# GpSimd's opening work in written order, and each q tile's scaling tied behind a spread, in a fused attention and expert kernel

## The chip, the cores and the metric

The kernel runs on one core of a Trainium2 chip. The metric is device microseconds of one execution: 626.1 us as the median of three runs (622.59, 626.1 and 626.88). The engines are called as the profile calls them: PE (TensorE), DVE (VectorE), ACT (ScalarE), POOL (GpSimd), and SP, whose queue issues most of the transfers.

## The reference

Three layers follow each other. Attention works on batch 2, 8 heads, 768 positions, head size 64, with a distance bias, a local window of 96 and 8 global keys:

```python
scores = scale * np.matmul(q, k.transpose(0, 1, 3, 2))
keep = is_global | is_local
scores = np.where(keep, scores + bias[None], -1000000000.0)
a = np.exp(scores - np.max(scores, axis=-1, keepdims=True))
a = a / (np.sum(a, axis=-1, keepdims=True) + 1e-09)
attn = np.matmul(a, v)                        # 1536 tokens x 512
h = x @ w_in                                  # 512 x 2048
x2 = (h * np.tanh(softplus(h))) @ w_out
...                                           # argmax routing over 8 experts
out[mask] = gate_w[mask, None] * (np.maximum(xe @ w1[e], 0.0) @ w2[e])
```

## The kernel before

**Tiles.** The 1536 tokens are 12 tiles of 128 (`t`), six per batch. Attention of a tile takes two steps (`s = 2t` and `2t + 1`), one for each four heads. The dense layer works on blocks of two tiles and pairs of weight columns; it is interleaved with attention from step 5 on, goes on alone until about 395 us, and the experts follow.

**One attention step.** `a_S` multiplies scaled q by k on PE (tile `sp`). `a_max` on DVE adds the distance bias `ndist` and finds the row maximum, `a_exp` on ACT takes the exponential and sums the rows into `su`, `a_T` transposes on PE (`pt`), `a_Tev` copies to SBUF on ACT (`PT`), and `a_V` multiplies by v on PE (`av`). After the second step of a tile, `a_recip` inverts the row sums on DVE (L315, L316) and POOL *spreads* them over 64 columns per head into the tile `rs` (L318). `a_R` transposes `rs` on PE (`rb`, L324), ACT copies it back (L325), and `a_x` multiplies `av` by it on DVE (L385), rounds it to `xh` on ACT (L386) and writes the rest `xl` on DVE (L387). There is one `rs` buffer: the spread of a tile can be written only when L387 of the tile before has read it.

**Scaling of q.** `prep_qk(t)` multiplies a q tile in place by a power of two per head (L261), which `a_S` of that tile needs. Tile 0 is done on DVE, tiles 1 to 11 on POOL. q is loaded for tile 0, tile 1, and from then on for two tiles at a time (tile name `qr`). In the program's text `prep_qk(t)` stands one step ahead of its `a_S`. For the first tile of each batch it also copies the global keys inside `kT` (L258, L259).

**Bias.** `ndist` is built on DVE (`bias_part`) in two pieces and completed by four copies on POOL (`bias_copies`, L98 to L101). The first two copies need the first piece, L100 and L101 the second.

**What sets the order.** A tile framework records the instructions and orders each engine's queue by a scheduler, from priorities and an estimate of readiness; each engine then runs its queue strictly in that order and waits on semaphores. A block under `tc.manual_schedule()` keeps the order of the text for the engines it covers; the opening (steps 0 to 4, with some repeated `warm` matmuls between, L839) is such a block. As built, POOL's work was not kept in that order: the scheduler had hoisted the scalings as early as their data could be ready. SP issues loads in its own order; many wait for a free slot of the six `st` buffers that q tiles and raw weights (`wst`) share, and a slot comes free when DVE has converted its weights (L165, L167, L169, into `cv`, then ACT's L203 and DVE's L205 into `wpair`).

Of the kernel before, what the change touches and what calls it, by code (L numbers as in the profile page):

```python
# [13 lines left out]
ALU = mybir.AluOpType  # L14
# [4 lines left out]
B, H, S, D = 2, 8, 768, 64  # L19
# [6 lines left out]
NL, NG = 96, 8  # L26
NPRE = NL + NG
WN = NPRE + 128
# [13 lines left out]
def moe_kernel(ctx, tc, q, k, v, n_global, n_local, w_in, w_out, w_gate, w1, w2, out, dbg=None):  # L42
    nc = tc.nc
# [45 lines left out]
    def bias_iota(nd, ci):  # L89
        ri = nd.bitcast(I32)  # L90
        nc.gpsimd.iota(ci, pattern=[[1, NG]], base=0, channel_multiplier=0)
        for c0, n, base_ in ((2 * WN, NG, 0), (2 * WN + NG, 128, 0), (0, NL, NL)):
            nc.gpsimd.iota(ri[:, c0:c0 + n], pattern=[[-1, n]], base=base_, channel_multiplier=1)
        nc.gpsimd.iota(ri[:, NL:NPRE], pattern=[[0, NG]], base=1 << 20, channel_multiplier=0)

    def bias_copies(nd):
        diag = nd[:, 2 * WN + NG:WC]
        nc.gpsimd.tensor_copy(nd[:, WN + NL:WN + NL + 128], diag)  # L98
        nc.gpsimd.tensor_copy(nd[:, NPRE:WN], diag)
        nc.gpsimd.tensor_copy(nd[:, WN:WN + NL], nd[:, 0:NL])  # L100
        nc.gpsimd.tensor_copy(nd[:, WN + NL + 128:2 * WN], nd[:, NL:NPRE])  # L101

    def bias_part(nd, gk, tmp, c0, w, gc):
        ri = nd.bitcast(I32)
# [23 lines left out]
    qsc = const.tile([128, 4], F32, name="qsc")  # L128
    cqs = const.tile([128, 1], F32, name="cqs")

    def build_scales():
        for p_ in range(4):
            nc.vector.memset(qsc[0:64, p_:p_ + 1], 2.0 ** (2 * p_ - 2))
            nc.vector.memset(qsc[64:128, p_:p_ + 1], 2.0 ** (2 * p_ - 1))
        nc.vector.memset(cqs, 2.0 ** -42)
# [79 lines left out]
    qkt = {}  # L215
# [7 lines left out]
    def load_qk(t, n=2):  # L223
        b, i = divmod(t, TPB)
        c0 = NG + (i // 2) * KB + (i % 2) * 128
        w = n * 128
        nc.sync.dma_start(kT[:, :, c0:c0 + w], k_t[:, :, t * 128:t * 128 + w])
        qr = stp.tile([128, 4, w], F32, tag="st", name="qr")
        nc.sync.dma_start(qr, q_t[:, :, t * 128:t * 128 + w])
        for j in range(n):  # L230
            qkt[t + j] = qr[:, :, j * 128:(j + 1) * 128]
# [21 lines left out]
    def prep_qk(t):  # L253
        i = t % TPB
        if i == 0:
            for j in range(1, 4):
                g0 = j * KB
                nc.gpsimd.tensor_copy(kT[:, :, g0:g0 + NG], kT[:, :, NG:2 * NG])  # L258
            nc.gpsimd.tensor_copy(kT[:, :, 0:NG], kT[:, :, NG:2 * NG])  # L259
        eng = nc.vector if t == 0 else nc.gpsimd  # L260
        eng.tensor_tensor(out=qkt[t], in0=qkt[t], in1=qsc.unsqueeze(2).to_broadcast([128, 4, 128]), op=ALU.mult)  # L261

    def geom(t):
        i = t % TPB
# [12 lines left out]
    rbs = {}  # L277
# [28 lines left out]
    def a_exp(s, q_):  # L306
        t, pr = divmod(s, 2)
        w = geom(t)[1]
        h = 4 * pr + q_
        nc.scalar.activation(out=Ps[s][:, q_, 0:w], in_=Ps[s][:, q_, 0:w], func=AF.Exp,  # L310
                             bias=mxs[s][:, q_:q_ + 1], scale=-1.0, accum_out=rcs[t][:, h:h + 1])

    def a_recip(t):
        su = rcs.pop(t)
        nc.vector.tensor_scalar_add(su, su, 1e-9)  # L315
        nc.vector.reciprocal(su, su)  # L316
        rbs[t] = at.tile([128, 4, 128], F32, tag="rs", name="rs", bufs=1)
        nc.gpsimd.tensor_copy(rbs[t].rearrange("p a (b c) -> p (a b) c", c=64),  # L318
                              su.unsqueeze(2).to_broadcast([128, H, 64]))

    def a_R(t):
        rb = ps.tile([128, 4, 128], F32, tag="b", name="rb")
# [492 lines left out]
    def next_raw():  # L815
        if nraw[0] < 32:
            load_raw(*chunks[nraw[0]])
            nraw[0] += 1
# [9 lines left out]
                    pass  # L828

    NS = 5  # L830
    with tc.manual_schedule(), tc.tile_pool(name="tmp0", bufs=1, side="right") as tmp0:
        build_scales()
        load_qk(0, 1)
        make_identity(nc, ident)
        warm = ps.tile([128, 512], F32, tag="b", name="warm")

        def fill(n_):
            for _ in range(n_):
                nc.tensor.matmul(warm[:, 0:128], lhsT=ident, rhs=ident, start=True, stop=True)  # L839

        fill(NWARM)
        ci = tmp0.tile([128, NG], I32, name="ci")
        bias_iota(ndist, ci)
        load_v(0)
        load_qk(1, 1)
        next_raw()
        load_v(1)
        load_qk(2)
        next_raw()
        next_raw()  # L850
        nl = make_int(nl_raw, "nl")
        ng = make_int(ng_raw, "ng")
        cf = tmp0.tile([128, NG], F32, name="cf")
        nc.vector.tensor_copy(cf, ci)
        gk = tmp0.tile([128, NG], F32, name="gk")
        nc.vector.tensor_scalar(out=gk, in0=cf, scalar1=ng, scalar2=None, op0=ALU.is_lt)
        for _ in bias_part(ndist, gk, tmp0, 2 * WN, NG + 128, 0):
            pass
        prep_qk(0)
        b1 = bias_part(ndist, gk, tmp0, 0, NPRE, NL)  # L860
        a_S(0)
        prep_qk(1)
        for q_ in range(4):
            a_max(0, q_)
        a_S(1)
        for s in range(NS):
            for q_ in range(2):
                a_exp(s, q_)
            if s:
                fill(4)  # L870
                a_T(s - 1, 0)
                a_T(s - 1, 1)
            if s and s + 1 < NS:
                a_S(s + 1)
            if s == 2:
                prep_qk(2)
            if s == 0:
                for _ in range(6):
                    next(b1, None)
            if s == 4:  # L880
                a_x(0)
            if s + 1 < NS:
                a_max(s + 1, 0)
                a_max(s + 1, 1)
            if s:
                a_Tev(s - 1, 0)
                a_Tev(s - 1, 1)
            if s in (2, 3):
                next_conv(1)
            for q_ in range(2, 4):  # L890
                a_exp(s, q_)
            if s + 1 < NS:
                a_max(s + 1, 2)
                a_max(s + 1, 3)
            if s == 0:
                for _ in range(6):
                    next(b1, None)
                bias_copies(ndist)
            if s in (1, 3):
                a_recip(s // 2)  # L900
            if s:
                fill(3)
                a_V(s - 1)
            if s in (2, 4):
                a_R(s // 2 - 1)
            if s in (2, 3):
                next_conv(2)
            if s in (1, 2):
                next_raw()
                next_conv(0)  # L910
            if s == 2:
                load_v(2)
            if s == 4:
                load_v(3)
        a_x(1)
        make_fast()
        build_consts(tmp0)
# [117 lines left out]
    for u in range(u0, NU + 2):  # L1035
        pl, bl, jl = units[u - 2]
        rt = bl - 1 if pl == 2 and bl > 0 else None
        if u < NU:
            p, b, j = units[u]
# [140 lines left out]
    with tc.If(slow > 0):  # L1180
        dense = nc.values_load(flag[0:1, 1:2], min_val=0, max_val=1)
        with tc.If(dense > 0):
            xd = dr.tile([NT, DM], F32, name="xd")
            sld = dr.tile([1, H], F32, name="sld")
            with tc.tile_pool(name="fa", bufs=1) as fa, tc.tile_pool(name="fap", bufs=1, space=PSUM) as fap:
# [13 lines left out]
                for b in range(B):  # L1199
                    with tc.For_i(0, H, 1) as hi_:  # L1200
# [10 lines left out]
                        for i in range(TPB):  # L1211
# [27 lines left out]
                            su = fa.tile([128, 1], F32, name="fsu")  # L1239
# [152 lines left out]
```

## Time and profile before

| | us |
|---|---|
| median of three runs | 626.1 |
| lowest and highest run | 622.59, 626.88 |
| the profiled execution | 625.67 |
| its span, first to last instruction | 623.9 |
| PE busy | 588.4 (94%) |
| DVE busy | 477.1 (76%) |
| ACT busy | 379.9 (61%) |
| POOL busy | 93.5 (15%) |

Busy times are of one profiled execution. In the 40 slices of the page, PE is at 9 tenths or more nearly everywhere from about 90 us on; the slices below that lie in the opening and where the experts begin. The mean clock granted to TensorE was 0.982 of full speed. A busy PE is not a PE at its peak: the record of a matmul also lasts longer when the granted clock is lower.

### The profile page before, as it was taken

What the parts mean: (1) busy time and instruction counts of PE and PEld (TensorE: products, weight loads), DVE (VectorE), ACT (ScalarE), POOL (GpSimd) and SP (SyncE); (2) the same over time, 40 slices, a digit from 0 to 9 for tenths busy, and PEclk for the clock granted to TensorE, in tenths of its full rate; (3) what the DMA queues carried; (4) which work ended last, traced back from release to release, by engine and by line L of the source; (5) the groups of instructions that cost most, each with busy time, mean ns of one, the idle gap of its engine ahead of it and who ended that gap; (6) DMA issues with size and microseconds to landing.
All of it is one profiled execution on the core that took longest, in us unless ns stands there. A gap on an engine that the chain in (4) does not pass through costs nothing.

```text
span 623.9 us, 12022 instructions
## 1 busy us (share of the span) xinstructions
PE 588.4 (94%) x4326; PEld 524.8 (84%) x4326; DVE 477.1 (76%) x1143; ACT 379.9 (61%) x882; POOL 93.5 (15%) x167
## 2 busy tenths in 40 slices
PE   7988799999999999999999999998999999999991
PEld 6766677777788999998989889788999999999990
DVE  5888899995579999877767677755985777988741
ACT  3659688977767666555555555555664566777630
POOL 2232120000100100000201111121310212221111
PEclk9979899999999999999999999999999999999996
DMA  7865656579959565441322210277667376568000
GB/s 216 296 187 185 200 187 231 207 246 285 271 192 319 177 217 188 136 136 35 103 92 78 86 52 34 98 251 270 209 222 256 107 270 229 174 241 301 28 17 20
DMA packets 54903, 109.93 MB, mean 176 GB/s; under 512 B 5707, under 2 KB 12875, under 8 KB 54834
## 3 DMA queue, kind: packets, MB, share of 16 engines
q1 hardware_dynamic: 49138, 90.18, 43.6%
q0 software_dynamic: 5696, 18.89, 9.1%
q8 instruction: 36, 0.59, 0.4%
q14 instruction: 33, 0.27, 0.1%
HBM read 84.64 MB, written 25.10 MB: 176 GB/s over the span
## 4 chain that ended last, share of the span: by engine, by line
PE 71%; DVE 9%; DMA 6%; ACT 6%; issue 4%; POOL 2%; SPq 0%; DVEq 0%; POOLq 0%; ACTq 0%
PE hp L418 22%; PE acc L437 18%; PE bhp L701 4%; PE bacc L701 4%; DMA bst<-in_moe_w_dram 3%; PE av L372 3%; PE bhp L702 2%; PE bacc L702 2%; DVE bw L155 2%; DMA xg<-x,dsi 1%; PE bhp L704 1%; PE bacc L704 1%; PE bacc L706 1%; PE bhp L706 1%; PE bacc L705 1%
## 5 line engine op out<-in xcount | busy, mean ns | idle before, releaser
L418 PE MATMUL hp<-xh,wpair 128*128 128x256 f32 x768 | 153.1, 289 | 3.3 <-ACT xh L386 3.3
L418 PEld LDWEIGHTS hp<-xh,wpair 128*128 128x128 f32 x768 | 123.4, 191 | 10.4 <-ACT xh L386 4.9
L437 PE MATMUL acc<-wpair,gh 128*128 128x512 f32 x384 | 123.1, 398 | 1.4 <-ACT gh L474 1.4
L418 PE MATMUL hp<-xl,wpair 128*128 128x256 f32 x384 | 111.9, 291 | 0.5 <-DVE xl L387 0.3
L437 PEld LDWEIGHTS acc<-wpair,gh 128*128 128x128 f32 x384 | 68.7, 188 | 16.5 <-issue 3.1
L155 DVE TENSOR_TENSOR bw<-bst,bw 128x512 fp32r<-128x512 f32 x112 | 72.9, 685 | 11.6 <-ACT bw L154 10.9
L445 ACT ACTIVATE e<-hp 128x512 f32<-128x512 f32 x48 | 28.7, 599 | 83.7 <-PE hp L418 83.6
L154 ACT CAST bw<-bst 128x512 fp32r<-128x512 f32 x112 | 64.3, 620 | 21.9 <-PE bhp L705 9.6
L437 PE MATMUL acc<-wpair,gl 128*128 128x512 f32 x192 | 76.9, 401 | 0.0
L418 PEld LDWEIGHTS hp<-xl,wpair 128*128 128x128 f32 x384 | 73.2, 191 | 3.2 <-DVE xl L387 1.4
L701 PE MATMUL bhp<-xc,bw 128*128 128x352 f32 (+4 forms) x192 | 59.4, 364 | 0.6 <-DVE t L736 0.5
L701 PE MATMUL bacc<-hc,bw 128*128 128x352 f32 (+4 forms) x192 | 59.3, 364 | 0.1
L310 ACT ACTIVATE P<-P,mx 128x232 f32<-128x232 f32 (+1 forms) x96 | 45.0, 470 | 18.0 <-DVE mx L299 18.0
L702 PE MATMUL bhp<-xc,bw 128*128 128x176 f32 (+4 forms) x192 | 48.4, 252 | 0.0
L702 PE MATMUL bacc<-hc,bw 128*128 128x176 f32 (+4 forms) x192 | 48.4, 252 | 0.0
L455 DVE SCALAR_TENSOR_TENSOR n<-n,r 128x512 f32<-128x512 f32 x48 | 33.6, 700 | 15.2 <-ACT r L453 15.1
L477 DVE SCALAR_TENSOR_TENSOR gl<-n,gh 128x512 fp32r<-128x512 f32 x48 | 33.6, 701 | 12.2 <-ACT gh L474 11.0
L437 PEld LDWEIGHTS acc<-wpair,gl 128*128 128x128 f32 x192 | 36.1, 188 | 7.3 <-DVE gl L477 0.2
L701 PEld LDWEIGHTS bhp<-xc,bw 128*128 128x128 f32 x192 | 36.1, 188 | 1.7 <-DVE t L736 0.7
L701 PEld LDWEIGHTS bacc<-hc,bw 128*128 128x128 f32 x192 | 36.1, 188 | 1.0 <-DVE hc L744 0.3
L702 PEld LDWEIGHTS bacc<-hc,bw 128*128 128x128 f32 x192 | 36.7, 191 | 0.0
L702 PEld LDWEIGHTS bhp<-xc,bw 128*128 128x128 f32 x192 | 36.7, 191 | 0.0
(190 smaller groups left out, 1252.0 us busy)
## 6 DMA issues: line engine op xcount, KB each, us to landing
bst<-in_moe_w_dram SPq DMA_DIRECT2D x56, 512.0 KB
wst<-in_moe_w_in_dram SPq DMA_DIRECT2D x16, 512.0 KB
wst<-in_moe_w_out_dram SPq DMA_DIRECT2D x16, 512.0 KB
xl<-xs POOLq DMA_DIRECT2D x12, 512.0 KB, 4.0
xh<-xs POOLq DMA_DIRECT2D x12, 512.0 KB, 4.7
xpl<-xps SPq DMA_DIRECT2D x24, 256.0 KB
xg<-z SPq DMA_DIRECT2D x24, 224.9 KB
w0f<-in_moe_w_dram SPq DMA_DIRECT2D x8, 512.0 KB
```

Source lines behind the costliest of these rows:

```text
L154: nc.scalar.copy(hi, src)
L155: nc.vector.tensor_sub(lo, src, hi.bitcast(F32))
L310: nc.scalar.activation(out=Ps[s][:, q_, 0:w], in_=Ps[s][:, q_, 0:w], func=AF.Exp, bias=mxs[s][:, q_:q_ + 1], scale=-1.0, accum_out=rcs[t][ ...
L372: nc.tensor.matmul(av[64 * j:64 * j + 64, 2 * pr + i, :], lhsT=lh, rhs=rh, start=(c == 0), stop=(c == 1))
L418: yield lambda f=f, kk=kk, wi=wi, xx=xx, cs=cs: nc.tensor.matmul(hp[:, f, :], lhsT=w[:, wi, kk, cs], rhs=xx[:, kk, :], start=(kk == 0 and ...
L437: yield lambda f=f, o=o, cs=cs, gi=gi, wi=wi, first=first, last=last: nc.tensor.matmul(accs[b][o], lhsT=gi[:, cs], rhs=w[:, wi, f, :], sta ...
L445: nc.scalar.activation(out=e, in_=hp, func=AF.Exp, scale=-1.0)
L455: nc.vector.scalar_tensor_tensor(out=n, in0=n, scalar=0.25, in1=r, op0=ALU.add, op1=ALU.mult)
L477: nc.vector.scalar_tensor_tensor(out=gl, in0=n, scalar=-(2.0 ** -80), in1=gh.bitcast(F32), op0=ALU.mult, op1=ALU.subtract)
L701: nc.tensor.matmul(o[:, 0:2 * cap], lhsT=wh, rhs=xc, start=first, stop=False)
L702: nc.tensor.matmul(o[:, 0:cap], lhsT=wl, rhs=xh, start=False, stop=last)
L704: nc.tensor.matmul(o[:, 0:cap], lhsT=wh, rhs=xh, start=first, stop=False)
```

## The change

Two things. The opening's `manual_schedule` now names PE, ACT, DVE and Pool, so POOL's instructions of the opening stand in the order of the text. And each scaling of a q tile from tile 3 on is traced in `tc.issue_after(...)`, which puts it on POOL's queue behind the instruction that `gorder` holds: the latest spread traced so far (`gorder` is first set to the last bias copy). No instruction is added or removed on any engine. PE, DVE and ACT have the same instructions in the same order. On SP one small load moves: `wg` (128x4x8 floats, 16 KB) now stands ahead of the k load of tiles 4 and 5 and no longer behind the first two stores to `xs`.

```diff
+    gorder = [None]
+
     def bias_copies(nd):
...
-        nc.gpsimd.tensor_copy(nd[:, WN + NL + 128:2 * WN], nd[:, NL:NPRE])
+        gorder[0] = nc.gpsimd.tensor_copy(nd[:, WN + NL + 128:2 * WN], nd[:, NL:NPRE]).ins
...
         eng = nc.vector if t == 0 else nc.gpsimd
-        eng.tensor_tensor(out=qkt[t], in0=qkt[t], in1=qsc.unsqueeze(2).to_broadcast([128, 4, 128]), op=ALU.mult)
+        with tc.issue_after(gorder[0]) if t > 2 else nullcontext():
+            eng.tensor_tensor(out=qkt[t], in0=qkt[t], in1=qsc.unsqueeze(2).to_broadcast([128, 4, 128]), op=ALU.mult)
...
-        nc.gpsimd.tensor_copy(rbs[t].rearrange("p a (b c) -> p (a b) c", c=64),
-                              su.unsqueeze(2).to_broadcast([128, H, 64]))
+        gorder[0] = nc.gpsimd.tensor_copy(rbs[t].rearrange("p a (b c) -> p (a b) c", c=64),
+                                          su.unsqueeze(2).to_broadcast([128, H, 64])).ins
...
-    with tc.manual_schedule(), tc.tile_pool(name="tmp0", bufs=1, side="right") as tmp0:
+    with tc.manual_schedule(engines={mybir.EngineType.PE, mybir.EngineType.Activation, mybir.EngineType.DVE, mybir.EngineType.Pool}), tc.tile_pool(name="tmp0", bufs=1, side="right") as tmp0:
```

The first place is POOL's queue in the opening, before the change. `qr_161` is the q load of tiles 2 and 3, `qr_568` that of tiles 4 and 5; `rs_286` and `rs_407` are the spreads of tiles 0 and 1.

```order
L98 COPY ndist_100<-ndist_100 128x128
L99 COPY ndist_100<-ndist_100 128x128
L261 TENSOR_TENSOR qr_161<-qr_161,qsc_95 128x4x128
L100 COPY ndist_100<-ndist_100 128x96
L101 COPY ndist_100<-ndist_100 128x8
L318 COPY rs_286<-su_212 128x512
L261 TENSOR_TENSOR qr_161<-qr_161,qsc_95 128x4x128
L261 TENSOR_TENSOR qr_568<-qr_568,qsc_95 128x4x128 x2
L318 COPY rs_407<-su_274 128x512
```

The same place now (line numbers are 2 or 3 higher in the changed file).

```order
L100 COPY ndist_100<-ndist_100 128x128
L101 COPY ndist_100<-ndist_100 128x128
L102 COPY ndist_100<-ndist_100 128x96
L103 COPY ndist_100<-ndist_100 128x8
L321 COPY rs_286<-su_212 128x512
L264 TENSOR_TENSOR qr_161<-qr_161,qsc_95 128x4x128
L321 COPY rs_407<-su_274 128x512
L140 MEMSET ones_89 128x128
L141 MEMSET tri_88 128x128
L264 TENSOR_TENSOR qr_161<-qr_161,qsc_95 128x4x128
```

The scaling of tile 2 moved from ahead of the last two bias copies to behind the spread of tile 0; the scalings of tiles 3, 4 and 5 no longer stand ahead of the spread of tile 1.

The second place is POOL's queue in the main loop, before the change: `qr_875` are tiles 6 and 7, `qr_1203` tiles 8 and 9, `qr_1520` tiles 10 and 11; the `rs` rows are the spreads of tiles 2 to 6.

```order
L318 COPY rs_589<-su_394 128x512
L258 COPY kT_104<-kT_104 128x4x8
L259 COPY kT_104<-kT_104 128x4x8
L261 TENSOR_TENSOR qr_875<-qr_875,qsc_95 128x4x128 x2
L318 COPY rs_742<-su_600 128x512
L258 COPY kT_104<-kT_104 128x4x8
L318 COPY rs_903<-su_753 128x512
L261 TENSOR_TENSOR qr_1203<-qr_1203,qsc_95 128x4x128 x2
L258 COPY kT_104<-kT_104 128x4x8
L261 TENSOR_TENSOR qr_1520<-qr_1520,qsc_95 128x4x128 x2
L318 COPY rs_1055<-su_914 128x512
L318 COPY rs_1224<-su_1066 128x512
```

The same place now.

```order
L321 COPY rs_589<-su_394 128x512
L264 TENSOR_TENSOR qr_568<-qr_568,qsc_95 128x4x128
L260 COPY kT_104<-kT_104 128x4x8
L261 COPY kT_104<-kT_104 128x4x8
L321 COPY rs_742<-su_600 128x512
L264 TENSOR_TENSOR qr_568<-qr_568,qsc_95 128x4x128
L260 COPY kT_104<-kT_104 128x4x8
L321 COPY rs_903<-su_753 128x512
L264 TENSOR_TENSOR qr_875<-qr_875,qsc_95 128x4x128
L260 COPY kT_104<-kT_104 128x4x8
L321 COPY rs_1055<-su_914 128x512
L264 TENSOR_TENSOR qr_875<-qr_875,qsc_95 128x4x128
```

The pairs of scalings came apart: one scaling stands behind each spread, that of tile t behind the spread of tile t - 2, and so on to tile 11 behind the spread of tile 9.

## Rows read from the trace of the kernel before

**Rows 1.** The page's first line.

```profile
span 623.9 us, 12022 instructions
```

**Rows 2.** Windows: length, then PE, PEld, DVE, ACT, POOL busy, clock, DMA share, GB/s.

```profile
15.00:20.00 5.00, 4.95 (x45) 3.69 (x43) 1.95 (x12) 1.78 (x8) 1.57 (x4) 1.00 1.05 374
20.00:25.00 5.00, 4.54 (x38) 3.17 (x40) 4.96 (x14) 2.96 (x10) 1.87 (x2) 1.00 0.55 168
...
30.00:35.00 5.00, 1.84 (x21) 1.17 (x20) 5.00 (x7) 2.54 (x7) 3.69 (x5) 0.99 0.42 152
35.00:40.00 5.00, 4.75 (x21) 3.67 (x21) 3.92 (x17) 3.29 (x9) 0.57 (x4) 0.50 0.81 256
...
110.00:120.00 10.00, 10.00 (x84) 7.89 (x82) 9.76 (x25) 8.59 (x24) 0.92 (x1) 1.00 0.38 127
...
200.00:300.00 100.00, 100.00 (x664) 90.70 (x664) 86.89 (x156) 58.76 (x101) 7.97 (x16) 1.00 0.45 147
```

**Rows 3.** The chain that ended last, in order of time: start, length, what.

```profile
32.53 1.48 POOL qr L261
...
57.82 1.03 POOL qr L261
```

**Rows 4.** Timeline of POOL: start, length, instruction, idle before and its releaser.

```profile
16.57 1.04 POOL L261 TENSOR_TENSOR qr<-qr,qsc 128x512 f32<-128x512 f32 x1 [5.15 <-DMA qr<-in_q_dram]
17.56 0.26 POOL L100 COPY ndist<-ndist 128x96 f32<-128x96 f32 x1
...
31.31 2.71 POOL L261 TENSOR_TENSOR qr<-qr,qsc 128x512 f32<-128x512 f32 x2 [9.44 <-DMA qr<-in_q_dram]
...
42.08 0.61 POOL L318 COPY rs<-su 128x512 f32<-128x512 f32 x1 [0.99 <-PE pt L337]
...
56.58 2.28 POOL L261 TENSOR_TENSOR qr<-qr,qsc 128x512 f32<-128x512 f32 x2 [6.06 <-DVE su L315]
...
82.23 2.49 POOL L261 TENSOR_TENSOR qr<-qr,qsc 128x512 f32<-128x512 f32 x2 [0.81 <-DMA qr<-in_q_dram]
...
99.88 0.87 POOL L318 COPY rs<-su 128x512 f32<-128x512 f32 x1 [10.93 <-DVE su L316]
```

**Rows 5.** Timeline of DVE.

```profile
13.58 0.27 DVE L119 TENSOR_TENSOR ndist<-loc,rel 128x104 f32<-128x104 f32 x1
...
17.98 0.40 DVE L299 CUSTOM_DVE_ANT_0 P<-sp,ndist 128x232 f32<-128x232 f32 x1 [4.14 <-POOL ndist L101]
...
30.99 0.69 DVE L387 TENSOR_TENSOR xl<-rs,xh 128x512 fp32r<-128x512 f32 x1
31.59 1.53 DVE L167 SCALAR_TENSOR_TENSOR cv<-wst,cv 128x512 int32<-128x512 int32 x1
...
45.65 0.43 DVE L447 TENSOR_SCALAR e<-e 128x512 f32<-128x512 f32 x1 [1.14 <-ACT e L445]
...
57.48 0.19 DVE L316 RECIPROCAL su<-su 128x8 f32<-128x8 f32 x1
...
61.70 0.40 DVE L299 CUSTOM_DVE_ANT_0 P<-sp,ndist 128x232 f32<-128x232 f32 x1 [1.15 <-PE sp L286]
```

**Rows 6.** One line's instructions in 0 to 60 us: minimum, median, maximum in ns.

```profile
L167 DVE SCALAR_TENSOR_TENSOR cv<-wst,cv x8: 677/737/1532, 20.0 to 49.7; 128x512 int32<-128x512 int32 x8
```

**Rows 7.** Timeline of PE.

```profile
31.33 1.36 PE L372 MATMUL av<-PT,vv 104*64 104x128 f32 x16 [0.98 <-ACT PT L350]
...
34.82 1.08 PE L324 MATMUL rb<-ident,rs 128*128 128x128 f32 x4 [2.13 <-POOL rs L318]
...
55.80 1.05 PE L286 MATMUL sp<-kT,qr 64*128 64x232 f32 x8
...
59.46 0.66 PE L324 MATMUL rb<-ident,rs 128*128 128x128 f32 x4 [1.60 <-POOL rs L318]
...
91.44 0.88 PE L372 MATMUL av<-PT,vv 128*64 128x128 f32 x12 [0.76 <-ACT PT L350]
...
113.76 1.05 PE L286 MATMUL sp<-kT,qr 64*128 64x232 f32 x8
```

## The prediction

> **What bounds the kernel now.** I read the windows first. From 110 us PE is busy in the whole of its time, and in 200 to 300 us it is busy 100.00 of 100 [rows 2]; whatever brings PE to that stretch earlier shortens the run by as much. In the opening it is different. In 30 to 35 us PE is busy 1.84 of 5, and in the next five its granted clock is 0.50, the lower of its two levels, 1.2 GHz [rows 2]. So the change has to be priced in the opening, from about 14 to 100 us.
>
> Next the chain of waits. It runs twice through POOL's scaling of q: at 32.53 us, and at 57.82 us [rows 3]. Both times the scaling stands ahead of a spread in POOL's queue, and PE waits for the spread: 2.13 us at 34.82 and 1.60 us at 59.46 [rows 7]. These scalings are of tiles 4 to 7, which nobody needs yet.
>
> Third, the timelines of POOL and DVE. At 16.57 POOL has waited 5.15 us for a q load; two small bias copies stand behind that, and DVE waits 4.14 us for them until 17.98 [rows 4, 5]. So three waits in the trace are of one kind: something short and urgent behind a scaling.
>
> The sum is made against the profiled execution, 625.67 us, of which the span is 623.9 [rows 1]; that run lies 0.4 us below the median of the three, 626.1.
>
> **The change part by part.** Nothing is added on an engine; eleven POOL scalings remain eleven.
>
> *Term A, the bias copies.* DVE has written the second bias piece at 13.58 + 0.27 = 13.85 us [rows 5]; the copies, which began at 17.56 [rows 4], can begin there, 3.7 us earlier. That is the upper end. But PE, with its warm matmuls in fixed order, is busy 4.95 of 5 and 4.54 of 5 in 15 to 25 us [rows 2]: it can gain only its idle time, 0.05 + 0.46 = 0.5 us. I take **0.5**, the PE end, because the next step of attention needs PE. What DVE gains beyond it is a head start for term B.
>
> *Term B, the spread of tile 1.* It follows the scalings of tiles 4 and 5, which take 31.31 to 34.02 [rows 4]. Now it only needs the buffer `rs`, free when DVE's L387 ends: 30.99 + 0.69 = 31.68 us [rows 5]. PE finishes `av` at 31.33 + 1.36 = 32.69 and waits until 34.82 [rows 7]; with the spread ready by then the whole **2.13** goes. That `av` had itself waited 0.98 us for ACT's copy of PT [rows 7], late because ACT had to wait for DVE before it; DVE's head start of term A should remove it too: **0.98** (ends 0 and 0.98).
>
> *Term C, the clock.* The clock fell right after these two waits of PE. In 35 to 40 us PE was busy 4.75 us at half speed [rows 2]; at full speed the same work takes 2.4, so up to 2.4 us come back, and nothing if DVE sets the pace. DVE is busy 3.92 of those 5 us [rows 2], and at 45.65 it waits 1.14 us for ACT, which had waited for the slow matmuls [rows 5]. I take **1.1**, what DVE itself waited.
>
> *Term D, the spread of tile 3.* The reciprocal is ready at 57.48 + 0.19 = 57.67 us [rows 5]; the spread had to let two scalings end at 56.58 + 2.28 = 58.86 [rows 4]. That is 1.2 us; PE's wait was 1.60, and DVE's for the scores behind it 1.15 at 61.70 [rows 5, 7]. I take **1.1** (ends 0 and 1.6).
>
> *Term E, what the scalings cost where they now stand.* While POOL scales, some DVE instructions take longer: L167 took 1.53 us beside the pair at 31.31, and 0.68 undisturbed [rows 5, 6]. One scaling therefore costs DVE between 0 and 0.85 us. Before, the pair of tiles 4 and 5 fell into PE's wait and cost nothing that counts. Now tiles 3, 4 and 5 follow spreads where DVE is nearly full: up to 2.6, of which DVE's remaining waits cover a part; I take **-1.0**. Tiles 6 to 11 fall later, tile 8 behind the spread at 99.88 [rows 4] and the last three beyond 110 us, where PE is full (10.00 of 10 busy, DVE 9.76 [rows 2]): I take 0 for these six, and keep -0.85 apiece for the lower end. In return the pair at 82.23, 2.49 us long [rows 4], no longer lies in front of DVE's work there; PE waited 0.76 us for ACT at 91.44, downstream of it [rows 4, 7]: **+0.76**.
>
> The SBUF page of the Trainium skill ("SBUF — State Buffer", section "Who interferes with whom") states that the port pair which DVE and GpSimd share is an exclusive lock: the second to issue is blocked for the whole first instruction if it has two SBUF inputs. This speaks against the change: by it every scaling behind a spread would cost DVE a whole scaling; the sum would lose what the third rival below works out. The 1.53 us agree with a lock in kind, but 0.85 is less than one scaling.
>
> *Terms of nothing.* The delayed scalings are hidden: tile 4 is scaled behind the spread at 42.08 + 0.61, so by about 43.8 with a 1.04 us scaling, and its scores start at 55.80; tile 8 behind the spread at 99.88 + 0.87, so by 101.8, scores at 113.76 [rows 4, 7]. Twelve microseconds of cover each; if it went, each late microsecond would be one of PE's. The `wg` load moves ahead of one k load on SP; that k is first read at 55.80 too, and `wg` not before routing. The key copies keep their places relative to the spreads, and other loads keep their order on SP.
>
> **Sum:** 0.5 + 2.13 + 0.98 + 1.1 + 1.1 - 1.0 + 0.76 = 5.6 us, so 625.67 - 5.6 = **620.1 us**.
>
> **The rivals.**
>
> *DVE is the real bound of the opening (chance 0.20).* For it: DVE is busy 5.00 of 5 in the very window where PE waits, 30 to 35 us [rows 2]. Against it: its instructions there are early work, stretched by the scalings. Then only DVE's own waits count: 1.08 in 35 to 40, 1.14 and 1.15 [rows 2, 5], together 3.4, less one more disturbed scaling than before, 0.85. Gain 2.5: 623.2 us.
>
> *PE is the bound throughout (0.15).* Then each cost of term E vanishes, C counts 2.4 and D 1.6: 0.5 + 2.13 + 0.98 + 2.4 + 1.6 + 0.76 = 8.4, so 617.3 us. For it: PE is full from 110 us on. Against it: ACT and DVE in between.
>
> *The scalings block DVE in full, and it comes out slower (0.06).* Nine scalings (tiles 3 to 11) then each hold up DVE by 1.04 us [rows 4], 9.4 in all, directly behind the reciprocal, where DVE has work. Of the old ones, four lay in DVE's dense part (tiles 8 to 11), at 0.85 each: 3.4 go. Net loss 6.0, against the 3.4 of DVE's own waits from the first rival: 2.6 slower, 628.3 us. It decides once DVE's delay per tile exceeds what DVE has to spare: 0.24 of 10 us in 110 to 120 [rows 2]. Against it: PE, not DVE, has the fuller record there. This is what the lock rule of the Trainium skill's SBUF page, named under term E, would make of the change.
>
> **How the numbers follow.** The forecast has 0.59, with 618 to 622.5 as its own range. A difference of 1% is 6.3 us, so the line against the median lies at 619.8 us, a hair from my sum; such a bound is about what a measurement of this kernel can tell from no change. Some 45% of the forecast's chance lies beyond it, 0.27, with the second rival's 0.15: faster 0.42. Same: the rest of the forecast, the first rival and most of the third, 0.55. Slower by over 1% would need the third rival at its worst: 0.03. The range reaches down to the edge of the second rival and up through the first: 617 to 625.
>
> **What would show it.** Right: `ndist` copies near 14 us and DVE's wait of 4.14 gone (A); the transposes of `rs` for tile 1 without a wait on POOL, before 32 us (B); clock 1.00 from 30 to 45 us (C); the next wait of PE on POOL at 59.46 gone (D). PE should reach its first dense matmul (L418) some 3.6 us earlier. What is late next: ACT's `xh`, which follows DVE's L385. Wrong: PE now waits as long for ACT or DVE in the same places; DVE's conversions last 1.5 us behind every spread; `a_S` waits on POOL; or the clock drops after another wait.

## The result and the profile after

The changed kernel takes 619.81 us (median of 17 runs, 616.71 to 624.35), the kernel before 625.2 us beside it (17 runs, 622.59 to 630.88). The ratio is 0.991, 95% interval 0.9888 to 0.9932: the 5.4 us are real, and a little less than the 1% that the prediction set as its line. The forecast was 620.1 us. Two slow runs of variants further down (711.92 us with only the engines named, at a mean clock of 0.75, and 629.04 us with tiles 3 to 5 tied) are in none of the medians and ratios.

The profiled execution of the changed kernel took 619.42 us. Its page and windows (length, busy us of PE, PEld, DVE, ACT and POOL, clock, DMA share, GB/s), to be laid beside [rows 1, 2]:

```profile
span 617.6 us, 12020 instructions
...
15.00:20.00 5.00, 5.00 (x47) 3.77 (x44) 4.55 (x16) 3.32 (x12) 2.07 (x2) 1.00 1.07 364
...
30.00:35.00 5.00, 2.23 (x21) 1.46 (x18) 3.05 (x9) 2.37 (x6) 3.70 (x7) 1.00 0.57 164
35.00:40.00 5.00, 5.00 (x48) 4.51 (x47) 4.97 (x22) 3.40 (x11) 1.86 (x3) 1.00 0.79 283
```

DVE works through 15 to 20 us, where it had waited; PE is full at full clock in 35 to 40 us, where it had run at 0.50. But in 30 to 35 us PE is still idle for more than half of the time. POOL's timeline tells why (start, length, instruction, idle before and its releaser):

```profile
13.97 0.27 POOL L102 COPY ndist<-ndist 128x96 f32<-128x96 f32 x1 [2.54 <-DVE ndist L121]
...
16.82 1.48 POOL L264 TENSOR_TENSOR qr<-qr,qsc 128x512 f32<-128x512 f32 x1
29.52 2.46 POOL L321 COPY rs<-su 128x512 f32<-128x512 f32 x1 [11.22 <-DVE xl L390]
...
32.23 1.04 POOL L264 TENSOR_TENSOR qr<-qr,qsc 128x512 f32<-128x512 f32 x1
...
38.33 0.62 POOL L321 COPY rs<-su 128x512 f32<-128x512 f32 x1 [0.88 <-DVE su L319]
38.90 1.48 POOL L264 TENSOR_TENSOR qr<-qr,qsc 128x512 f32<-128x512 f32 x1
...
53.62 0.61 POOL L321 COPY rs<-su 128x512 f32<-128x512 f32 x1 [6.33 <-DVE su L319]
```

The bias copies stand at 14 us and each spread goes ahead of its scaling (that at 16.82 is tile 2's, long done when the spread of tile 1 starts), against [rows 4]. The new thing is the third row: the spread of tile 1 starts as soon as its buffer is free, with nothing in front of it, and lasts 2.46 us; the spreads at 38.33 and 53.62 last 0.61. DVE's timeline of the same microseconds, and the rows that answer to [rows 5]:

```profile
14.40 0.40 DVE L302 CUSTOM_DVE_ANT_0 P<-sp,ndist 128x232 f32<-128x232 f32 x1 [0.57 <-ACT PT L353]
...
29.29 0.68 DVE L169 SCALAR_TENSOR_TENSOR cv<-wst,cv 128x512 int32<-128x512 int32 x1
29.89 0.41 DVE L167 TENSOR_SCALAR cv<-wst 128x512 int32<-128x512 int32 x1
30.23 0.68 DVE L171 SCALAR_TENSOR_TENSOR cv<-wst,cv 128x512 int32<-128x512 int32 x1
30.83 0.68 DVE L169 SCALAR_TENSOR_TENSOR cv<-wst,cv 128x512 int32<-128x512 int32 x1
33.40 0.69 DVE L388 TENSOR_TENSOR rs<-av,rs 128x512 f32<-128x512 f32 x1 [1.90 <-ACT rs L328]
...
39.40 1.52 DVE L207 TENSOR_TENSOR wpair<-cv,wpair 128x512 fp32r<-128x512 f32 x1
```

DVE runs four weight conversions back to back from 29.29 to 31.51 us, none of them stretched, and the spread ends 0.47 us after the last, at 31.98. PE's timeline shows who pays:

```profile
29.29 1.10 PE L375 MATMUL av<-PT,vv 104*64 104x128 f32 x16
...
32.03 0.66 PE L327 MATMUL rb<-ident,rs 128*128 128x128 f32 x4 [1.65 <-POOL rs L321]
...
34.80 0.38 PE L421 MATMUL hp<-xh,wpair 128*128 128x256 f32 x1 [1.12 <-ACT xh L389]
...
43.71 0.44 PE L375 MATMUL av<-PT,vv 104*64 104x128 f32 x4 [1.15 <-ACT PT L353]
...
54.29 0.66 PE L327 MATMUL rb<-ident,rs 128*128 128x128 f32 x4 [0.63 <-POOL rs L321]
...
60.05 0.58 PE L421 MATMUL hp<-xh,wpair 128*128 128x256 f32 x1 [2.53 <-ACT xh L389]
```

The wait of 2.13 us [rows 7] is still there with 1.65, and DVE waits 1.90 us behind it at 33.40. In the chain of waits of the changed kernel (start, length, what) the spread has taken the scaling's place of [rows 3]:

```profile
29.52 2.47 POOL rs L321
```

By how much PE is earlier than before, in the two profiled executions (one of each kernel, both with the granted clock at 1.00 in 10 to 12 us):

| PE starts | before | after | earlier |
|---|---|---|---|
| scores of step 2 | 12.75 | 12.83 | -0.08 |
| scores of step 4 | 24.77 | 23.78 | 0.99 |
| transposes of `rs`, tile 1 | 34.82 | 32.03 | 2.79 |
| first dense matmul | 38.01 | 34.80 | 3.21 |
| scores of step 8 | 55.80 | 51.59 | 4.21 |
| scores of step 9, second part | 61.01 | 55.84 | 5.17 |
| scores of step 10 | 72.18 | 68.25 | 3.93 |
| scores of step 13 | 93.59 | 87.65 | 5.94 |
| transposes of `rs`, tile 11 | 170.87 | 165.50 | 5.37 |
| wait for `gh` near the end of the dense layer | 405.14 | 399.76 | 5.38 |
| end of the span | 623.9 | 617.6 | 6.3 |

### The profile page after: what moved, and what is told of

Same layout as the page of the kernel before. It is cut to its first block, busy times and chain, and to the rows that moved or that the text cites. A ratio compares the mean times of both kernels' runs of the same rounds, so it can differ in the third digit from the quotient of the medians.

```text
span 617.6 us, 12020 instructions
## 1 busy us (share of the span) xinstructions
PE 585.2 (95%) x4326; PEld 523.5 (85%) x4326; DVE 474.7 (77%) x1143; ACT 379.8 (61%) x882; POOL 93.9 (15%) x167
## 4 chain that ended last, share of the span: by engine, by line
PE 76%; DVE 7%; ACT 6%; DMA 5%; issue 3%; POOL 1%; SPq 0%; DVEq 0%; POOLq 0%; ACTq 0%
PE hp L421 23%; PE acc L440 18%; PE bhp L704 5%; PE bacc L704 5%; PE av L375 3%; PE bhp L705 2%; PE bacc L705 2%; DMA bst<-in_moe_w_dram 2%; DMA xg<-z 2%; PE sp L289 2%; ACT P L313 2%; PE warm L842 1%; PE bhp L707 1%; PE bacc L707 1%; PE bacc L709 1%
```

## The experiments

In all of them the kernel before ran on the same chip beside the variant, which has 4 to 10 runs. Beside the ratio of times with its interval stand three numbers of one profiled execution each, which need not be near the median: how long after the start of DVE's `xl` of tile 0 (L387 before, L390 now), which frees `rs`, the transposes of tile 1 begin on PE; when PE's matmul that waits for `gh` starts; and how long the spread of tile 1 lasts.

| kernel | median us | ratio [95%] | `xl` to transposes | `gh` wait | spread of tile 1 |
|---|---|---|---|---|---|
| before | 625.2 | 1 | 3.83 | 405.14 | 0.80, behind a pair |
| changed | 619.81 | 0.9910 [0.9888, 0.9932] | 3.34 | 399.76 | 2.46 |
| changed, again | 619.74 | 0.9911 [0.9882, 0.9939] | 3.37 | 400.42 | 2.46 |
| only the engines named | 625.94 | 1.0015 [0.9994, 1.0037] | 5.34 | 407.19 | 0.61, behind a pair |
| tile 3 tied | 625.24 | 1.0012 [0.9987, 1.0038] | 5.33 | 405.21 | 0.61, behind a pair |
| tiles 4, 5 tied | 623.42 | 0.9984 [0.9959, 1.0010] | 1.81 | 402.44 | 0.91 |
| tiles 3 to 5 tied | 621.8 | 0.9947 [0.9917, 0.9977] | 3.34 | 399.07 | 2.46 |
| scaled twice | 622.12 | 0.9949 [0.9924, 0.9975] | 3.35 | 402.25 | 2.46 |
| spread 1 on ACT | 617.71 | 0.9889 [0.9856, 0.9923] | 2.26 | 398.26 | 0.61, on ACT |
| fewer warm | 615.93 | 0.9887 [0.9835, 0.9939] | 1.81 | 398.12 | 0.91 |
| fewer warm, again | 618.29 | 0.9894 [0.9862, 0.9926] | 3.36 | 398.38 | 2.45 |
| fewer warm, spread on ACT | 618.25 | 0.9891 [0.9844, 0.9937] | 2.28 | 396.15 | 0.61, on ACT |
| no warm | 618.04 | 0.9874 [0.9846, 0.9902] | 3.35 | 400.35 | 2.45 |
| warm in step 9 | 619.18 | 0.9912 [0.9883, 0.9940] | 3.35 | 400.44 | 2.46 |

The column of `xl` sorts them: 1.81 where the spread lasts 0.91, 2.26 to 2.28 where ACT does it, 3.34 to 3.37 where it lasts 2.45 or 2.46, 5.3 where a pair of scalings that DVE holds up stands ahead of it, and 3.83 in the profile of before, where the pair got in between DVE's conversions.

**Which half of the change acts.** The naming of the engines alone, with no scaling tied:

```diff
-        with tc.issue_after(gorder[0]) if t > 2 else nullcontext():
+        with nullcontext():
```

> The other half of the change alone: the opening's manual schedule names its four engines, and no scaling is tied. GpSimd's queue comes out as it was before; only the wg load moves on SP's queue. Theory (naming the engines does nothing on GpSimd and wg's load is hidden): 624 to 626, ratio 1.000 within its interval, DVE's wait of 4.14 us and PE's of 2.13 us stay. Rival (the early wg load disturbs the full transfers of 8 to 20 us): 0.3% or more slower, later landings of q and raw weights.

It did nothing (1.0015). POOL's order in this kernel is that of before, the scaling ahead of the bias copies and the pair ahead of the spread. Its timeline, then rows of DVE's and PE's:

```profile
16.44 1.04 POOL L264 TENSOR_TENSOR qr<-qr,qsc 128x512 f32<-128x512 f32 x1 [5.04 <-DMA qr<-in_q_dram]
17.42 0.26 POOL L102 COPY ndist<-ndist 128x96 f32<-128x96 f32 x1
...
32.55 3.03 POOL L264 TENSOR_TENSOR qr<-qr,qsc 128x512 f32<-128x512 f32 x2 [10.80 <-DVE cv L167]
35.52 0.61 POOL L321 COPY rs<-su 128x512 f32<-128x512 f32 x1
```

```profile
32.99 0.68 DVE L169 SCALAR_TENSOR_TENSOR cv<-wst,cv 128x512 int32<-128x512 int32 x1
38.01 0.69 DVE L388 TENSOR_TENSOR rs<-av,rs 128x512 f32<-128x512 f32 x1 [4.33 <-ACT rs L328]
```

```profile
36.19 1.11 PE L327 MATMUL rb<-ident,rs 128*128 128x128 f32 x4 [3.62 <-POOL rs L321]
```

DVE's wait at 18 us stays (4.04), as expected, but PE's is 3.62 where the profile of before has 2.13. Here the pair ends 1.91 us after the last of DVE's four conversions (35.58 against 33.67), none of which is stretched; in the profile of before the pair got in between and stretched one to 1.53 [rows 5]. One order of the queue thus met with either result.

So the effect needs the tying of the scalings. The other kernels keep the naming of the engines; the tie without the naming wasn't run.

**Term by term.** Only some tiles are tied; the three conditions, one for each kernel:

```diff
-        with tc.issue_after(gorder[0]) if t > 2 else nullcontext():
+        with tc.issue_after(gorder[0]) if t == 3 else nullcontext():
+        with tc.issue_after(gorder[0]) if t in (4, 5) else nullcontext():
+        with tc.issue_after(gorder[0]) if t in (3, 4, 5) else nullcontext():
```

> Only the scaling of tile 3 is tied behind a spread; it was the one that stood ahead of the last two bias copies. The scalings of tiles 4 and 5 stay ahead of the spread of tile 1. Theory (bias copies are worth little because PE is full there; the spreads carry the gain): DVE's wait of 4.14 us at 18 us goes, PE's fourth score block starts about 1.0 us earlier, PE's wait for the spread of tile 1 at 34.82 us stays or grows to 3 us, and the time is 624.5 to 625.5, under 0.2% from before. Rival (DVE's head start is the gain): 621 to 622.5, half of the change or more.

> Only the scalings of tiles 4 and 5 are tied behind spreads; tile 3 still stands ahead of the bias copies. Theory: PE's 2.13 us wait for the spread of tile 1 shrinks to about 1.5 (DVE now locks the spread out for a while), the clock stays at 1.00 from 35 to 42 us, and the time is 621.5 to 623.5: 2 to 3.5 us of the 5.6. Rival (bias copies carry it): 624 to 625.5.

> Tiles 3, 4 and 5 are tied, 6 to 11 stay hoisted in pairs. Theory (terms A to C alone, without the moved scalings of tiles 6 to 11): the opening up to 53 us is as in the changed kernel; PE's wait for the spread of tile 3 (1.60 us before) comes back, DVE instructions of 1.2 to 1.5 us return near 75 and 80 us; 621 to 622.5. Rival (the scalings behind spreads cost DVE time in 88 to 142 us): faster than the changed kernel, 618 to 619.5.

With tile 3 alone the bias copies come at 13.96 us, and nothing is gained (1.0012). The timelines of POOL, PE and DVE of that kernel:

```profile
30.12 4.49 POOL L264 TENSOR_TENSOR qr<-qr,qsc 128x512 f32<-128x512 f32 x2 [10.93 <-DVE cv L167]
34.56 0.61 POOL L321 COPY rs<-su 128x512 f32<-128x512 f32 x1
...
35.42 1.04 POOL L264 TENSOR_TENSOR qr<-qr,qsc 128x512 f32<-128x512 f32 x1
```

```profile
35.22 1.11 PE L327 MATMUL rb<-ident,rs 128*128 128x128 f32 x4 [3.63 <-POOL rs L321]
```

```profile
32.04 0.68 DVE L169 SCALAR_TENSOR_TENSOR cv<-wst,cv 128x512 int32<-128x512 int32 x1
37.04 0.69 DVE L388 TENSOR_TENSOR rs<-av,rs 128x512 f32<-128x512 f32 x1 [4.33 <-ACT rs L328]
```

DVE's wait at 18 us is gone. But it waits 4.33 us at 37 us, as it does with only the engines named, and there too the pair ends 1.9 us after DVE's last conversion (34.61 against 32.72): these waits aren't brought by the tie. Against that execution, whose opening is the nearest (granted clock 0.50 in 10 to 12 us, here 0.64), `xl` starts 0.96 us earlier (29.89 against 30.85) and the transposes 0.97; why this isn't in the time isn't shown. The expected 1.0 us at the fourth score block didn't come: the scores of step 4 start at 24.98, against 24.77 before and 24.91 with only the engines named. This kernel shows also that the scaling ahead of the bias copies is tile 3's: tying tile 3 moves it away (now 35.42).

Tiles 4 and 5 alone give nothing in the time that can be told from none (0.9984, interval to 1.0010), though here the 2.13 us of term B went in full. PE's timeline of that kernel:

```profile
31.30 1.37 PE L375 MATMUL av<-PT,vv 104*64 104x128 f32 x16 [0.98 <-ACT PT L353]
32.77 0.66 PE L327 MATMUL rb<-ident,rs 128*128 128x128 f32 x4
```

The spread starts at 31.80 and lasts 0.91, and the transposes wait for nobody; `av` waits its 0.98 us as before [rows 7], and DVE still waits 4.06 us at 18 us. Tiles 3 to 5 together give 0.9947, more than the two parts' 1.0012 and 0.9984. That suggests that the two waits stand one behind the other and that their removal pays together, but the excess over the two parts, 0.005, is hardly larger than the noise of the three ratios together, so it isn't shown. As expected, PE waits again for the spread of tile 3, which here stands behind a pair: 1.60 us at 55.18, against 0.63 in the changed kernel. Whether tiles 6 to 11 add the rest, up to 0.991, isn't settled: the intervals touch, and in the trace this kernel is at the `gh` wait 0.7 us ahead of the changed one and loses 3.2 us in the expert stage after it (end of span 620.1), where no scaling is. Its granted clock there was 0.57 in 404 to 408 and in 428 to 432 us, against 1.00 in both in the changed kernel.

**What a scaling costs where it now stands.** Each scaling from tile 3 on is followed by a second one, by ones, also on POOL:

```diff
+            if t > 2:
+                eng.tensor_tensor(out=qkt[t], in0=qkt[t], in1=qone.unsqueeze(2).to_broadcast([128, 4, 128]), op=ALU.mult)
```

> The changed kernel, with each scaling of tiles 3 to 11 followed by a second multiplication by 1.0 on GpSimd: nine more instructions of about 1.04 us, each right behind a scaling. Theory (outside tiles 3 to 5 PE covers the disturbance of DVE): 0 to 1.5 us slower than the changed kernel, 620 to 621.5. Rival (each blocks DVE in full and DVE sets the pace): 5 to 9 us slower, 625 to 629.

622.12 us, 2.3 us above the changed kernel for nine more scalings: 0.26 us apiece. The two intervals overlap (0.9924 to 0.9932), so the size is loose. The time lies between the two expectations. The scalings neither leave DVE alone nor hold it up each time: of the 128x512 instructions of DVE up to 180 us that are recorded one by one, 8 last more than 1.1 us in this kernel and 3 in the changed one (6 before).

**Whether the 2.46 us of the spread are DVE's doing.** The spread of tile 1 is done by ACT, ahead of the transposes; all other spreads stay on POOL. The scaling tied to it moves to the spread of tile 0 (20.69 us).

```diff
+        if t == 1:
+            late[0] = su
+            return
...
     def a_R(t):
+        if t == 1:
+            rbs[t] = at.tile([128, 4, 128], F32, tag="rs", name="rs", bufs=1)
+            nc.scalar.copy(rbs[t].rearrange("p a (b c) -> p (a b) c", c=64),
+                           late[0].unsqueeze(2).to_broadcast([128, H, 64]))
```

> The changed kernel with the spread of tile 1 alone done by ScalarE, traced just ahead of its transposes. In the changed kernel that spread lasted 2.46 us on GpSimd beside four VectorE instructions with two SBUF operands, against 0.61 undisturbed, and PE waited 1.65 us. Theory (GpSimd was locked out of the shared port by VectorE): on ScalarE it lasts 0.5 to 0.7 us beside the same VectorE instructions, the transposes start near 31.0 us, 1.0 us earlier than in the changed kernel, and VectorE's instructions in that stretch keep 0.68 us. Rival (the spread is slow because its input or the buffer rs comes late): it ends near 32 us there too. The scheduler reorders later ScalarE work in this kernel, so its total may move by 2 us either way, 617 to 622.

The timelines of ACT and DVE of this kernel, over the same conversions:

```profile
32.73 0.61 ACT L332 COPY rs<-su 128x512 f32<-128x512 f32 x1
```

```profile
31.73 0.68 DVE L169 SCALAR_TENSOR_TENSOR cv<-wst,cv 128x512 int32<-128x512 int32 x1
32.33 0.42 DVE L167 TENSOR_SCALAR cv<-wst 128x512 int32<-128x512 int32 x1
32.67 0.68 DVE L171 SCALAR_TENSOR_TENSOR cv<-wst,cv 128x512 int32<-128x512 int32 x1
33.27 0.68 DVE L169 SCALAR_TENSOR_TENSOR cv<-wst,cv 128x512 int32<-128x512 int32 x1
```

On ACT the same copy takes 0.61 us beside the same four conversions (three of which read two tiles; L167 reads one), so neither the data nor the buffer makes it long; that DVE's run held POOL up is read from this and from the pair of executions below. From `xl` to the transposes it is 2.26 us, against 3.34 in the changed kernel: 1.08 us shorter. Counted from the start of the span the transposes come at 33.39 and not near 31.0 as expected, because the opening of this execution was late: its granted clock was 0.50 in 10 to 15 us, and the scores of step 2 start at 15.04. In the whole time this isn't secured: 617.71 against 619.81, and the intervals overlap.

**The warm matmuls.** PE runs repeated matmuls that compute nothing between the opening's steps; in steps 1 to 4 they are cut to one before the transposes and one before `av`, and in another kernel taken out:

```diff
-                fill(4)
+                fill(1)
                 a_T(s - 1, 0)
...
-                fill(3)
+                fill(1)
                 a_V(s - 1)
```

> The changed kernel with 2 instead of 7 warm matmuls per step of the opening, 20 fewer in steps 1 to 4, each about 0.13 us of PE. Theory (PE with its warm matmuls, not DVE, set the pace from 13 to 30 us, so that DVE's head start of 3.6 us gave PE only 1.0): the transposes of tile 1's spread start 1 to 2.5 us earlier than 32.03 us, and the time is 617 to 619.5 unless PE's clock falls in the gaps. Rival (ScalarE or VectorE set the pace there): no earlier, 620 or more; or a granted clock of 0.50 in 20 to 40 us and 621 to 624.

> One warm matmul in place of four and of three in steps 1 to 4, scalings as in the changed kernel. Theory (the warm matmuls stand in TensorE's path of the opening and cost 2 us there): 615.5 to 618.5 us, ratio 0.984 to 0.989, below the changed kernel of the same job by 0.3 to 0.6%. Rival (what was seen was a favourable execution): 618.5 to 621 us, no difference from the changed kernel.

The two profiled executions of this one program show who locked out whom. In the first, POOL's timeline and DVE's:

```profile
29.76 0.91 POOL L321 COPY rs<-su 128x512 f32<-128x512 f32 x1 [9.96 <-DVE xl L390]
```

```profile
29.53 0.68 DVE L169 SCALAR_TENSOR_TENSOR cv<-wst,cv 128x512 int32<-128x512 int32 x1
30.13 0.83 DVE L167 TENSOR_SCALAR cv<-wst 128x512 int32<-128x512 int32 x1
30.88 0.68 DVE L171 SCALAR_TENSOR_TENSOR cv<-wst,cv 128x512 int32<-128x512 int32 x1
```

The second, in the same order:

```profile
28.27 2.45 POOL L321 COPY rs<-su 128x512 f32<-128x512 f32 x1 [9.97 <-DVE xl L390]
```

```profile
28.02 0.69 DVE L169 SCALAR_TENSOR_TENSOR cv<-wst,cv 128x512 int32<-128x512 int32 x1
28.63 0.42 DVE L167 TENSOR_SCALAR cv<-wst 128x512 int32<-128x512 int32 x1
28.96 0.69 DVE L171 SCALAR_TENSOR_TENSOR cv<-wst,cv 128x512 int32<-128x512 int32 x1
29.56 0.69 DVE L169 SCALAR_TENSOR_TENSOR cv<-wst,cv 128x512 int32<-128x512 int32 x1
```

Where L167 took 0.83 instead of 0.42 us, the spread got in behind L169 and lasted 0.91; where DVE went on undisturbed, the spread waited for all of them. In the first the spread ends 0.46 us after the end of the first L169 (30.67 against 30.21), in the second 0.47 after the end of the last one (30.72 against 30.25). From `xl` to the transposes it is 1.81 against 3.36 us: the 1.55 are the difference of the two spreads. The cut of the warm matmuls itself is seen with an equal spread: the scores of step 2 start at 12.83 us in the second execution and in the changed kernel's first, the transposes at 30.78 against 32.03, 1.25 us earlier. Little of that lasted: the clock stood at 0.50 in 30 to 34 us, and at the scores of step 6 PE was at 39.95 us against 40.06. In the time the cut isn't secured either: 0.9894 beside 0.9911 for the changed kernel of the same job, where 0.3 to 0.6% less was expected.

> As the kernel before it in this list, and the spread of tile 1 on ScalarE, ahead of its transposes. Theory (the lock-out of GpSimd's spread is worth 1 us on TensorE's path by itself): 614 to 617 us, about 1 us below the kernel with fewer warm matmuls alone. Rival (with fewer warm matmuls the spread falls beside other work of DVE and lasts 0.9 us, so that nothing is left to take): 615.5 to 618.5 us, the same as it.

With both edits it is 2.28 us from `xl` to the transposes, as with the copy on ACT alone, and the `gh` wait comes at 396.15, the earliest of all. But that execution (613.52) is the second shortest of six, which lay between 613.29 and 621.82, so that the median, 618.25, is no better than that of the cut alone, 618.29: the expected further microsecond isn't shown.

The other variant takes out both `fill` lines:

```diff
-                fill(4)
...
-                fill(3)
```

> No warm matmuls at all in steps 1 to 4. Theory (their time is pure loss on the path): the transposes of tile 1 another 0.6 to 1 us earlier, 614.5 to 617 us. Rival (they hold the granted clock): the clock falls to 0.50 somewhere between 12 and 35 us, and the time is 618 to 622 us.

The theory missed on both counts: the transposes of tile 1 start at 32.14, later than the 30.73 and 30.78 with fewer warm matmuls, and the time is 618.04. The rival came out by the letter, with the granted clock at 0.50 in 12 to 15 and 30 to 38 us and a time at the lower edge of its range, but the kernel lost nothing by it. Its ratio is the lowest of its group, 0.9874 [0.9846, 0.9902], against 0.9911 [0.9882, 0.9939] for the changed kernel beside it: some 1.7 us faster, and overlapping.

The opposite edit adds 18 warm matmuls where PE waits 2.53 us for `xh` at 60 us:

```diff
+            if s == 9:
+                warm2 = ps.tile([128, 512], F32, tag="b", name="warm2")
+                for _ in range(18):
+                    nc.tensor.matmul(warm2[:, 0:128], lhsT=ident, rhs=ident, start=True, stop=True)
```

> The changed kernel with 18 warm matmuls (2.4 us of PE) in front of the dense matmuls that wait 2.53 us for xh at 60 us, after which the profiled execution had its clock at 0.50 from 60 to 66 us. Theory (the wait costs a stretch at the lower clock, about 1 us of the end): the clock stays at 1.00 from 58 to 70 us, the tenth step's scores start about 1.5 us earlier than 68.25 us, and the time is 618 to 619.5. Rival (VectorE sets the pace there, and some executions keep the clock anyway): 619.5 to 621.

The clock stayed at 1.00 through 58 to 70 us, and the step from the scores of step 9 to those of step 10 took 11.13 us against 12.41; the time was 619.18, no change that can be told. That doesn't price the clock: in the changed kernel's second execution it was 1.00 there without the added matmuls, and the same step took 9.91 us.

**The changed kernel once more.**

> The changed kernel as it is, beside the three that follow. 618.5 to 621 us, ratio to before 0.989 to 0.993. The spread of tile 1 lasts about 2.5 us beside DVE's operations, and S1 to the transposes of tile 1 takes 19.2 us.

The windows of the changed kernel's first and second profiled execution:

```profile
10.00:12.00 2.00, 2.00 (x22) 1.52 (x18) 1.78 (x13) 1.54 (x8) 1.43 (x5) 1.00 1.07 298
34.00:38.00 4.00, 3.20 (x28) 2.96 (x30) 3.95 (x24) 3.65 (x11) 0.19 (x1) 1.00 0.96 374
62.00:66.00 4.00, 4.00 (x20) 3.45 (x20) 4.00 (x7) 1.84 (x4) 2.06 (x2) 0.50 0.91 314
```

```profile
10.00:12.00 2.00, 2.00 (x15) 1.75 (x13) 1.90 (x14) 1.66 (x8) 1.55 (x5) 0.55 1.08 293
34.00:38.00 4.00, 3.46 (x17) 2.77 (x16) 3.28 (x15) 3.27 (x9) 0.83 (x4) 0.51 0.84 319
62.00:66.00 4.00, 3.29 (x26) 2.83 (x26) 4.00 (x9) 3.23 (x10) 0.23 (x1) 1.00 0.98 347
```

The same program kept its clock at 34 us and lost it at 62 in one execution, and the other way round in the next. By the scores of step 9 the second was 2.64 us behind the first (58.48 against 55.84), by those of step 10 0.14, and the times were 619.42 and 619.82.

This second execution also has a partner in POOL's order of before: the one with only the engines named, whose clock was likewise low in 10 to 12 us (0.50, here 0.55). Between these two PE gains 0.01 us at the scores of step 4 (24.91 to 24.90), 3.03 at the transposes of tile 1, 3.27 at the scores of step 8 and 6.77 at the wait for `gh`, where the table above has 0.99, 2.79, 4.21 and 5.38. The gain as a whole is there in both pairs; a single term is known from such profiles to one or two microseconds at best.

## Why the prediction was right, point by point

The total was right, 5.6 us forecast and 5.4 measured, and so was the picture: three short, urgent things behind scalings that nobody needed yet. The terms were less exact than the total, and that it came within 0.2 us is in part luck: B gave 0.9 us less than forecast, A half a microsecond more, and the -1.0 of E didn't show. Of the signs that the prediction named, that of B failed (the transposes of tile 1 at 32.03, with a wait on POOL), and one for "wrong" came in: the clock dropped after another wait, to 0.50 in 62 to 66 us.

*Term A* (0.5 taken, 0.5 to 3.7). The bias copies came at 13.97 as forecast, and the wait of 4.14 us went. PE was 0.99 us earlier at step 4, about twice the idle time that was taken as the limit. That isn't so in every execution: with the lower clock in 10 to 12 us the scores of step 4 start at 24.90 in the changed kernel's second one, and at 24.91 with only the engines named, where the bias copies are as late as before. And tile 3 tied by itself gave nothing in the time. The prediction called the scalings ahead of spread 1 those of tiles 4 and 5, which holds; the text ahead of it gave the one ahead of the bias copies to tile 2, and it is tile 3's. That text also gives the order of POOL's opening to the naming of the engines, which alone moves nothing on POOL. Neither touched the sum.

*Term B* (2.13 + 0.98) is the step that was mis-sized. The 0.98 went, as said: `av` at 29.29 has no wait, and PE gains another 1.05 us between step 4 and there (31.33 - 29.29 - 0.99). Of the 2.13 only 0.48 went, since the new wait is 1.65: together 2.22 us up to the first dense matmul (3.21 - 0.99), 3.11 forecast. The prediction held the spread to be ready by 31.68 plus its 0.6 us; the buffer was indeed free earlier still, near 29.4. What failed was the spread's length: it was taken to be short because nothing stood ahead of it on its own engine, and beside DVE's conversions it took 1.85 us more (2.46 - 0.61). The two executions of one program with fewer warm matmuls show this directly: 0.91 or 2.45 us, with 1.81 or 3.36 from `xl` to the transposes. Up to the first dense matmul A and B gave 3.21 us, 3.6 forecast.

The prediction had the mechanism in hand, but in one direction: a scaling on POOL that stretches DVE. What bit was the other direction, DVE's conversions stretching a spread on POOL; with tiles 4 and 5 tied alone, where the spread got in, the 2.13 did go in full. The Trainium skill's page "SBUF — State Buffer", section "Who interferes with whom", says that the issue order decides which of the two is blocked. The prediction used its rule only for a VectorE instruction that comes second, behind a scaling; the page's condition, a VectorE instruction with two SBUF inputs beside a GpSimd instruction that reads SBUF, holds for a spread that comes second as well. That one of the two is held up, and either can be, the two executions above bear out. That the issue order decides they don't show: by its recorded start the spread comes 0.23 and 0.25 us after the first L169 and ahead of L167 in both, and it lasts 0.91 in one and 2.45 in the other. The page speaks of a block for one instruction; the 2.46 us here span what is left of a run of four.

*Term C* (1.1, 0 to 2.4). From the first dense matmul to step 8 PE gained 1.00 us more, with the clock at 1.00 in 30 to 44 us as forecast. The bound by DVE's own wait fits: with full clock PE then waited 1.15 us for ACT's `PT` at 43.71. But the second execution had the clock at 0.51 in 34 to 38 us and the same time in the end. The term is thus no secure part of the gain.

*Term D* (1.1). The wait of 1.60 fell to 0.63, and PE gained 0.96 us; with tiles 3 to 5 tied, where the pair stands ahead of this spread, the 1.60 are there again. The rest of the wait is about the spread's own length, 0.61, behind the reciprocal.

*Term E* (-1.0 + 0.76). The -1.0 was for tiles 3 to 5, whose scalings lie ahead of step 9. With it A to D would give 4.8 us up to there, and PE gained 5.17, so most of that cost didn't come. Between step 9 and the wait for `gh` the balance is 5.38 - 5.17 = +0.21 us, against the +0.76; the path differs between executions by the clock (3.93 at step 10, then 5.94 at step 13). The scaling of tile 3 cost nothing, because it fell into DVE's new wait of 1.90; that of tile 4 stretched L207 to 1.52. Doubling all nine scalings cost 0.26 us each, less than the 0.85 of the lower end.

*Terms of nothing.* PE's scores waited for no late scaling up to 110 us: the waits there are for `xh` (3.7 us), `rs` (2.3) and `PT` (1.4). The late next was ACT's `xh`, as said.

The last 0.9 us, from 5.38 at the `gh` wait to 6.3 at the end, lie in the expert stage. From that wait to the end of the span it took 218.8 us before, 217.8 and 217.7 in the two executions after, 221.0 with tiles 3 to 5 tied, and 215.7 to 220.5 in the other kernels. The 0.9 us lie within that scatter. No step of the prediction speaks of it, no instruction of the change stands there, and it stays open.

*The rivals.* DVE as the bound would have left PE's waits in other places and 623.2 us; part of it is seen in PE's waits for `rs` and `xh`, but DVE has a wait of 1.90 us of its own in the middle. PE as the bound throughout would have paid the clock in full. The scalings as a full block of DVE, slower, is refuted by the time, and by the second scaling's price of 0.26 us.

## What to carry to other kernels

When something urgent is freed on GpSimd's queue, look at what VectorE does in the microseconds into which it moves: a short copy with nothing ahead of it took four times its length beside back-to-back VectorE work, and none of that showed in the trace of before. Waits that may stand one behind the other on two engines are best removed and priced together: here the parts gave 1.0012 and 0.9984, and both 0.9947. And compare the same landmarks in a second execution, of the kernel before as well as of the changed one, before a clock's rise or a moved wait is booked to a term.

## What the runs showed of the hardware that was not expected

- The same four VectorE conversions and the same GpSimd copy met with either result: the copy lasted 0.91 us and L167 0.83, or the copy 2.45 and L167 0.42, in two executions of one program. In 0.91 us of copy VectorE lost 0.41; in 2.45 it lost nothing. In all nine profiles with the spread of tile 1 on GpSimd and nothing ahead of it, the copy starts 0.23 to 0.25 us after the first of the four and ends 0.46 to 0.48 us after the end of one of them: of the first in two profiles, of the last in seven. A pair of scalings took 4.49 us in the same way where the profile of before has 2.71.
- After a wait of TensorE of about 1.8 to 2.0 us, which ends at 9.3, the granted clock in 10 to 12 us was 1.00 in one execution of the changed kernel and 0.55 in another, and the scores of step 2 started at 12.83 and 13.96. Of its next waits, 1.65 us (up to 32.03 and 33.16) and 2.53 us (up to 60.05 and 62.71), one execution has the clock at 0.50 after the second, the other at 0.51 after the first.
- The opening without its warm matmuls had the clock at 0.50 in 30 to 34 us and 0.67 on the mean of 30 to 44, and the kernel was no slower for it.
